# One Trainium2 core, mLSTM and a mixture of experts: other zero products ahead of the first expert step, chunk 2 read and normed ahead of the fourth step

## The chip, the cores and the metric

The kernel runs on one core of a Trainium2 chip. The metric is the time of one execution in microseconds (us). The engines' names are those of the profile: PE is TensorE (PEld its weight loads), DVE is VectorE, ACT is ScalarE, POOL is GpSimd, SP is the engine that issues the DMA transfers here.

## The reference: what is computed

Two parts in a row, all float32. The first is an mLSTM over batch 2, 8 heads, 768 positions, head size 40, written as a recurrence:

```
m_new = maximum(f_t + m, i_t)
f_stab, i_stab = exp(f_t + m - m_new), exp(i_t - m_new)
C = f_stab * C + i_stab * outer(v_t, k_t);  n = f_stab * n + i_stab * k_t
y_t = sigmoid(o_t) * (C q_t) / maximum(|n . q_t|, 1)
```

The second takes the result as 1536 tokens of width 320 and sends every token through 4 experts with hidden width 1024:

```
p = domain_probs / (domain_probs.sum(-1) + 1e-9)
out = sum over e of p[:, e] * (maximum(x @ w1[e], 0) @ w2[e])
```

## The kernel before, in words

The sequence is cut into 12 chunks of 128 tokens; chunk `n` is batch `n % 2`, position block `n // 2`. In a chunk the recurrence is matrix work:

- `scores(n)` (L447): k times q on TensorE, into two PSUM tiles `s`. `decay(n)` (L416): two DVE scans that make the decay matrix `dd` from a broadcast of the forget gates, `fb`. For chunks 0 to 3 `fb` is made on TensorE into PSUM by `spread(n)` (L399); from chunk 4 on it is loaded into SBUF from a DRAM copy by `load_f(n)` (L409). `weigh(n)` (L453, DVE): scores times decay, `pm`.
- `inter(n)` (L494): q times the state `cs` carried from the chunk before, into a PSUM tile, and 8 ACT copies `yb` (L501). `intra(n)` (L509): `pm` times the values `vp`, into another. `norm(n)` (L522 to L529, DVE): adds both, divides and gates.
- `state(n)` (L465): the chunk's addition to the state; `carry(n)` (POOL, L481) decays the old one, L475 (DVE) adds. `values(n)` (L428 ACT, L430 POOL) and `keys(n)` (L436 POOL) make its operands.
- `turn(n)` (L536): three transposes, and ACT copies (L538, L539) into the experts' input `xst`; `turn_lo(n)` (L543, L544, DVE) the rests.

Float32 products of the experts are made from parts in a shorter format: each weight and each input is split into a high part (`split_hi`, L96, ACT) and a low rest (`split_lo`, L99, POOL or DVE), and TensorE adds up products of the parts.

The first of the 4 experts runs while the attention does. The class `Expert` holds a list of steps for a group of 256 tokens: 4 steps `hidden` (L164: 16 products into one PSUM bank, then relu and rest, L173 and L174) and then the steps `output` (L203). For the first group the output of each of its two token blocks is cut in two: the part with the high half of `w2` (16 products) and the part with the low half (8 products), in the order high 0, high 1, low 0, low 1. `steps(n)` runs the next `n` steps. The order of everything is written out by hand: each engine takes its instructions in the order of the code, and waits by semaphores only. `SLOTS` gives, for each chunk from 2 on, how many steps run before `inter(n + 1)`, before `turn(n)` and after `turn_lo(n)`.

The code from L554 to L676 is a prelude for chunks 0 and 1. It begins with the gates: scans and exponentials on 16 partitions; `gate_t` (L329) transposes them with TensorE, `gate_b` (L306) is a long DVE scan, `gate_last` and `gate_l` (L351) give the factors `bl` (L355) for the carried states. The first four `hidden` steps are spread over the prelude, L643, L649, L665 and L674. The loop from L678 does chunks 2 to 11.

`keep_warm(n)` (L75) is a product of 128 x 128 zeros with `n` columns of zeros; nothing reads it.

PSUM tiles come from pools of two buffers taken in turn. `gate_t`, `intra`, `inter`, `state` and the later `turn` share the pool `ps_y`: each takes the buffer that the tile two before it had, and waits until that one has been read. The scores and some zero products share `ps_w`. The SBUF pool `a0` for the loaded `fb` takes the place of the gates' pool `gp` (L668), tile by tile when the gates have been read.

Of the kernel before, what the change touches and what calls it, by code (L numbers as in the profile page):

```python
# [10 lines left out]
AF = mybir.ActivationFunctionType  # L11
# [7 lines left out]
L = 128  # L19
# [16 lines left out]
NPE = 4  # L36

SLOTS = (
    (0, 1, 1), (1, 1, 0), (0, 2, 0), (1, 1, 0), (1, 1, 0),
    (1, 1, 0), (1, 1, 0), (1, 1, 0), (1, 2, 0), (1, 1, 1),  # L40
)
PAD = 56
# [6 lines left out]
def tile_mlstm_moe(ctx, tc, gt, qk, vk, ot, dp, w1, w2, out):  # L49
    ctx.enter_context(tc.manual_schedule())  # L50
    nc = tc.nc
# [20 lines left out]
    def keep_warm(n, pool=ps_h, tag="ph"):  # L72

        pwm = pool.tile([L, n], F32, tag=tag, name="pwm")
        nc.tensor.matmul(pwm, zero[:, 0:L], zero[:, 0:n], start=True, stop=True)  # L75

    for _ in range(WARM):
        keep_warm(512)
    keep_warm(256)

    def copy(eng, dst, src):
        if eng is nc.scalar:
            eng.activation(dst, src, AF.Copy)
        else:
            eng.tensor_copy(dst, src)
# [9 lines left out]
    def split_hi(hi, raw):  # L95
        nc.scalar.activation(hi, raw, AF.Copy)  # L96
# [11 lines left out]
    def split_w2_hi(ws, f0, n, raw):  # L108
        f = slice(f0, f0 + n)
        split_hi(ws[:, HI, f], raw[:, f])  # L110
# [111 lines left out]
    with ExitStack() as actx:  # L222
# [4 lines left out]
        w1s, w2s = new_weights(0)  # L227
# [24 lines left out]
        ps_y = actx.enter_context(tc.tile_pool(name="ps_y", bufs=2, space=PSUM))  # L252
# [4 lines left out]
        BH = B * H  # L257
        gat = gp.tile([BH, 2, S], F32, name="gat")
# [4 lines left out]
        ib = gp.tile([L, S], F32, name="ib")  # L263
# [55 lines left out]
        def gate_t(c0, c1):  # L319

            pit = pits[c0] = ps_y.tile([L, 512], F32, tag="y", name="pit")
            n = c1 - c0
            po = n * 48
            if c0:
                g = slice(c0 * L, c1 * L)
                nc.scalar.activation(ib[32:32 + BH, g], gat[:, 0, g], AF.Copy)
            for c in range(c0, c1):
                o = (c - c0) * 48
                nc.tensor.matmul(  # L329
                    pit[:, o:o + 48], ib[:, c * L:(c + 1) * L], ident[:, 0:48],  # L330
                    start=True, stop=True,
                )
            nc.scalar.activation(
                ibT[:, c0:c1], pit[:, 0:po].rearrange("t (c g) -> t c g", c=n), AF.Copy
            )
# [77 lines left out]
        def decay(n):  # L413
            dds[n] = a1.tile([L, H, L], F32, tag=f"dd{n % 2}", name="dd")
            for i in range(2):
                nc.vector.tensor_tensor_scan(  # L416
                    out=dds[n][:, 4 * i:4 * i + 4].rearrange("p h t -> p (h t)"),
                    data0=fbs[n][i].rearrange("p h t -> p (h t)"),
                    data1=id4.rearrange("p h t -> p (h t)"),
                    initial=0.0, op0=ALU.mult, op1=ALU.add,  # L420
                )
# [19 lines left out]
        def scores(n, pool=ps_w, tag="w"):  # L441
            ss[n] = [pool.tile([L, NP, L], F32, tag=tag, name="s") for _ in range(2)]
            qg, kg = qT(n), kT(n)
            for p in range(NP):
                for r in range(2):
                    q = slice(64 * r, 64 + D * r)
                    nc.tensor.matmul(ss[n][r][:, p, :], kg[q, p], qg[q, p], start=True, stop=True)  # L447
# [29 lines left out]
        def carry(n):  # L477
            b, c = n % B, n // B
            if 0 < c < NC - 1:
                cd = cds[n] = a1.tile([104, NP, L], F32, tag=f"cd{b}", name="cd")  # L480
                nc.gpsimd.tensor_mul(  # L481
                    cd, cs[b][0:104],
                    bl[0:104, c, b * NP:(b + 1) * NP].unsqueeze(2).to_broadcast([104, NP, L]),
                )

        def inter(n, pool=ps_y, tag="y"):

            b, c = n % B, n // B
            if c == 0:
                return  # L490
            y1 = pool.tile([L, H, 64], F32, tag=tag, name="y1")
            for p in range(NP):
                for t in (slice(0, 64), slice(64, L)):
                    nc.tensor.matmul(  # L494
                        y1[t, 2 * p:2 * p + 2, :].rearrange("t r d -> t (r d)")[:, 0:65 + D],
                        qT(n)[:, p, t], cs[b][0:104, p, 0:65 + D], start=True, stop=True,
                    )
            yb = ybs[n] = a1.tile([L, H, D + 1], F32, tag=f"yb{n % 2}", name="yb")
            for h in range(H):
                i = 32 + b * H + h  # L500
                nc.scalar.activation(  # L501
                    yb[:, h], y1[:, h, 0:D + 1], AF.Copy, scale=ibT[:, c, i:i + 1]
                )

        def intra(n):
            y = y0s[n] = ps_y.tile([L, H, 64], F32, tag="y", name="y0")
            for h in range(H):
                for t in (slice(0, 64), slice(64, L)):
                    nc.tensor.matmul(  # L509
                        y[t, h, 0:D + 1], pms[n][:, h, t], vvs[n][:, h, 0:D + 1],  # L510
                        start=True, stop=True,
                    )

        def norm(n):

            y, xr = y0s[n], a1.tile([L, H, D], F32, tag=f"xr{n % 2}", name="xr")
            xrs[n] = xr.rearrange("t h d -> t (h d)")
            yd, yn = y[:, :, 0:D], y[:, :, D:D + 1]
            nq = a1.tile([L, H, 1], F32, tag="nq", name="nq")
            na, ni = y[:, :, D + 2:D + 3], y[:, :, D + 4:D + 5]  # L520
            if n // B:
                nc.vector.tensor_add(y[:, :, 0:D + 1], y[:, :, 0:D + 1], ybs[n])  # L522
            nc.vector.tensor_scalar(
                out=nq, in0=yn, scalar1=-1.0, scalar2=1.0, op0=ALU.mult, op1=ALU.max
            )
            nc.vector.tensor_mul(xr, yd, ogs[:, n])  # L526
            nc.vector.tensor_tensor(out=na, in0=yn, in1=nq, op=ALU.max)
            nc.vector.reciprocal(ni, na)
            nc.vector.tensor_mul(xr, xr, ni.to_broadcast([L, H, D]))  # L529
# [18 lines left out]
        def steps(n):  # L548
            for _ in range(n):
                if not work[0].step():  # L550
                    work.pop(0)
# [36 lines left out]
        nc.scalar.activation(even, par.unsqueeze(2).to_broadcast([L, 2, 64]), AF.Copy)  # L588
        gate_max(1, NC)
        spread(0, ps_h, "ph")  # L590
        for _ in range(2):
            keep_warm(256, ps_w, "w")
        scores(0)
        gate_t(0, 1)
# [1 line left out]
        g1, m1, mp1 = slice(L, S), mb[:, L + 1:S + 1], mb[:, L:S]  # L596
# [5 lines left out]
        decay(0)  # L602
        nc.gpsimd.tensor_sub(fs[:, g1], fs[:, g1], m1)
        nc.scalar.activation(fs[:, g1], fs[:, g1], AF.Exp)
        scores(1, ps_h, "ph")
        weigh(0)
        decay(1)
# [6 lines left out]
        w2r = raws.tile([L, NF, DM], F32, tag="raw", name="w2r")  # L614
        nc.sync.dma_start(w2r, w2[0])
        load_vk(1)
        load_o(1)
        for _ in range(3):
            keep_warm(256, ps_w, "w")
        weigh(1)  # L620
        quarter_hi(0)
# [19 lines left out]
        gate_b(1, NC)  # L641
        gate_last(1, NC)
        steps(1)  # L643
        decay(2)
        scores(2)
        state(0)
# [18 lines left out]
        steps(1)  # L665
        gate_l(1, NC)
        carry(2)
        gctx.close()  # L668
        a0 = actx.enter_context(
            tc.tile_pool(name="a0", bufs=1, side="right", reuse_waits="tile")  # L670
# [2 lines left out]
        load_f(NPE + 1)  # L673
        steps(1)  # L674
        nc.vector.reciprocal(psum_e, psum_e)
        inter(2)  # L676

        for n in range(2, NCH):  # L678
            j, cc = n // 2, n % 2
            k = SLOTS[n - 2]  # L680
            nxt = n + 1 < NCH
            if cc == 0 and j + 1 < NG:
                load_qk(j + 1)
                load_vk(j + 1)
            if NPE + 1 < n + 2 < NCH:
                load_f(n + 2)
            if cc == 0:
                if j > 1:
                    gate_o(j)
                if j + 1 < NG:  # L690
                    load_o(j + 1)
            if n == NCH - 2:
                raw1 = load_w1e(1)
            if n > 3 and nxt:
                decay(n + 1)
            steps(k[0])
            if nxt:
                inter(n + 1)
            intra(n)
            norm(n)  # L700
            if n == 2:
                for f in (4, 6):
                    split_w2_hi(w2s, f, 2, w2r)
            if nxt:
                scores(n + 1)
            state(n)
            if nxt:
                values(n + 1)
                if n == 2:
                    for f in (4, 6):  # L710
                        split_w2_lo(w2s, f, 2, w2r, nc.gpsimd)
                    nc.gpsimd.tensor_mul(pw, pw, psum_e.to_broadcast([L, NCH, NE]))
                keys(n + 1)
                weigh(n + 1)
                carry(n + 1)
            steps(k[1])
            turn(n)
            if n == 2:
                decay(4)
            turn_lo(n)  # L720
            steps(k[2])
# [109 lines left out]
```

## Time and profile before

| | |
|---|---|
| time, median of 3 runs | 411.47 us (408.71 to 411.73) |
| the profiled execution | 413.55 us |
| its span, first to last instruction | 411.7 us |
| TensorE busy | 402.6 us (98%) |
| DVE, ACT, POOL busy | 174.1, 125.4, 85.0 us |
| mean granted clock of TensorE | 0.988 |
| relu copies L173 on ACT, 96 of them | 598 ns mean |

Times in the views are counted from the start of the span. The granted clock is the share of TensorE's full speed that was granted in a stretch: 1.00 or, at its lower level, 0.50. In the chain of waits every piece is what the end of the program was waiting for at that time: an engine with the operation and its line, a transfer, or "issue", which is time in which the engine waited for nothing that the profile shows. In the timelines a bracket after a row gives how long the engine had been idle before it and what released it. "x16" is the number of instructions merged in a row; a product of float32 data is recorded as two.

### The profile page before, as it was taken

How to read it: one execution, taken by the hardware profiler on the slowest of the kernel's cores; microseconds unless marked ns; L12 is line 12 of the kernel's file. 1: busy time of each engine (PE TensorE's matmuls, PEld its weight loads, DVE VectorE, ACT ScalarE, POOL GpSimd, SP SyncE). 2: the span in 40 equal slices, each digit the busy share in tenths (PEclk: the TensorE clock that was granted, in tenths of full speed). 3: DMA queues.
4: the chain of work that ended last, by engine and by line, in shares of the span. 5: the costliest groups of instructions: out<-in, count | busy, mean ns of one | idle time of the engine just before them, and what ended most of it. 6: DMA issues, size and time to landing. Idle time of an engine off the chain costs nothing.

```text
span 411.7 us, 7167 instructions
## 1 busy us (share of the span) xinstructions
PE 402.6 (98%) x3046; PEld 365.3 (89%) x3046; DVE 174.1 (42%) x312; ACT 125.4 (30%) x298; POOL 85.0 (21%) x97
## 2 busy tenths in 40 slices
PE   8989999999999999999999999999999999999996
PEld 5778989999998898998988988989989889899896
DVE  7683699699762403313214234133142251231321
ACT  4657434353323533205214032033030140220210
POOL 4865932222012620003410010016100010000000
PEclk9698999999999999999999999999999999999999
DMA  6964967545000213000300004002000000001001
GB/s 174 306 228 110 240 175 222 150 134 206 2 2 2 77 52 116 37 2 0 129 0 2 0 2 153 2 0 90 40 0 2 0 2 32 33 0 49 17 18 48
DMA packets 14883, 29.34 MB, mean 71 GB/s; under 512 B 987, under 2 KB 10747, under 8 KB 13435
## 3 DMA queue, kind: packets, MB, share of 16 engines
q1 hardware_dynamic: 14851, 28.88, 22.3%
q8 instruction: 24, 0.39, 0.4%
q14 instruction: 8, 0.07, 0.1%
HBM read 26.86 MB, written 2.02 MB: 70 GB/s over the span
## 4 chain that ended last, share of the span: by engine, by line
PE 94%; DMA 2%; DVE 1%; issue 1%; SPq 1%; ACT 0%; ACTq 0%
PE po L203 41%; PE ph L164 40%; PE y L509 3%; PE s L447 3%; PE ph L186 3%; DMA qk<-in_qk 2%; PE y L494 2%; PE st L465 1%; PE px L536 1%; PE pwm L75 1%; PE pit L329 0%; SPq L555 0%; PE fb L399 0%; DVE pm L453 0%; DVE xr L526 0%
## 5 line engine op out<-in xcount | busy, mean ns | idle before, releaser
L203 PE MATMUL po<-w2s,h 128*128 128x320 f32 x1152 | 172.8, 310 | 0.0
L203 PEld LDWEIGHTS po<-w2s,h 128*128 128x128 f32 x1152 | 169.7, 188 | 1.0
L164 PE MATMUL ph<-xst,w1s 128*128 128x512 f32 (+1 forms) x816 | 165.6, 361 | 0.0
L164 PEld LDWEIGHTS ph<-xst,w1s 128*128 128x128 f32 x816 | 137.2, 191 | 24.8 <-issue 2.4
L173 ACT ACTIVATE h<-ph 128x512 fp32r<-128x512 f32 x96 | 57.4, 598 | 200.6 <-PE ph L164 200.6
L174 DVE SCALAR_TENSOR_TENSOR h<-ph,h 128x512 fp32r<-128x512 f32 x96 | 66.2, 689 | 104.0 <-ACT h L173 103.5
L213 DVE SCALAR_TENSOR_TENSOR acc<-po,pw,acc 128x320 f32<-128x320 f32 x36 | 19.8, 550 | 99.9 <-PE po L203 99.9
L99 POOL TENSOR_TENSOR w1s<-raw,w1s 128x512 fp32r<-128x512 f32 (+1 forms) x24 | 23.6, 1023 | 74.4 <-ACT w1s L96 67.4
L99 POOL TENSOR_TENSOR w2s<-raw,w2s 128x640 fp32r<-128x640 f32 x6 | 9.5, 1577 | 98.2 <-ACT w2s L96 98.2
L416 DVE TENSOR_TENSOR_SCAN dd<-fb,id 128x512 f32<-128x512 f32 x24 | 28.0, 1208 | 1.8 <-PE fb L399 1.6
L211 ACT ACTIVATE acc<-po,pw 128x320 f32<-128x320 f32 x12 | 6.3, 528 | 34.7 <-PE po L203 34.7
L501 ACT ACTIVATE yb<-y,ibT 128x41 f32<-128x41 f32 x80 | 15.8, 317 | 2.6 <-PE y L494 2.2
L447 PE MATMUL s<-qk 64*128 64x128 f32 x192 | 14.9, 297 | 1.5 <-DMA qk<-in_qk 1.5
L453 DVE TENSOR_TENSOR pm<-s,dd 128x512 f32<-128x512 f32 x24 | 15.4, 686 | 1.4 <-PE s L447 1.1
L509 PEld LDWEIGHTS y<-vp,pm 128*64 128x64 f32 x384 | 13.3, 145 | 3.0 <-issue 2.1
L509 PE MATMUL y<-vp,pm 128*64 128x41 f32 x384 | 14.0, 235 | 1.7 <-issue 1.0
L447 PEld LDWEIGHTS s<-qk 64*128 64x128 f32 x192 | 12.5, 199 | 2.5 <-PE pwm L75 1.1
L436 POOL TENSOR_TENSOR kp<-vk,dd 128x320 f32<-128x320 f32 x10 | 8.2, 827 | 29.5 <-DVE dd L416 29.5
L96 ACT ACTIVATE w2s<-raw 128x640 fp32r<-128x640 f32 x12 | 8.8, 733 | 16.2 <-DMA raw<-in_w 16.2
L186 PE MATMUL ph<-xd,w1s 64*128 64x512 f32 x40 | 12.0, 420 | 0.0
L186 PE MATMUL ph<-xst,w1s 64*128 64x512 f32 x40 | 11.9, 417 | 0.0
L430 POOL TENSOR_TENSOR vp<-vk,ibT 128x320 f32<-128x320 f32 x12 | 8.7, 724 | 13.9 <-PE st L465 9.0
(90 smaller groups left out, 205.8 us busy)
## 6 DMA issues: line engine op xcount, KB each, us to landing
raw<-in_w SPq DMA_DIRECT2D x3, 1536.0 KB, 6.4
qk<-in_qk SPq DMA_DIRECT2D x5, 832.0 KB
fb<-f_d SPq DMA_DIRECT2D x8, 512.0 KB, 3.9
raw<-in_w SPq DMA_DIRECT2D x3, 1280.0 KB
vk<-in_vk SPq DMA_DIRECT2D x5, 640.0 KB, 8.2
acc<-in_ot SPq DMA_DIRECT2D x6, 320.0 KB, 8.1
out<-acc SPq DMA_DIRECT2D x12, 160.0 KB, 1.8
w2r<-in_w SPq DMA_DIRECT2D x1, 1280.0 KB
```

The lines of the kernel that those rows point to most:

```text
L99: eng.tensor_sub(lo, raw, hi.bitcast(F32))
L164: nc.tensor.matmul(ph[:, i, :], self.w1s[:, wi, f * L:(f + 1) * L], xst[:, xi, self.t0:self.t0 + n], start=(k == 0 and not self.wide), sto ...
L173: nc.scalar.activation(hh, ph, AF.Relu)
L174: nc.vector.scalar_tensor_tensor(out=hl, in0=ph, scalar=0.0, in1=hh.bitcast(F32), op0=ALU.max, op1=ALU.subtract)
L186: nc.tensor.matmul(self.banks[f][:, 0, :], self.w1s[r, 5, f * L:(f + 1) * L], x, start=True, stop=False,)
L203: nc.tensor.matmul(po, self.hs[f][a][:, sl], ws[:, b, f, :], start=(first and i == 0), stop=(last and i == len(ks) - 1),)
L213: nc.vector.scalar_tensor_tensor(out=acc[:, i, :], in0=po, scalar=pw[:, i, e:e + 1], in1=acc[:, i, :], op0=ALU.mult, op1=ALU.add,)
L416: nc.vector.tensor_tensor_scan(out=dds[n][:, 4 * i:4 * i + 4].rearrange("p h t -> p (h t)"), data0=fbs[n][i].rearrange("p h t -> p (h t)") ...
L447: nc.tensor.matmul(ss[n][r][:, p, :], kg[q, p], qg[q, p], start=True, stop=True)
L453: nc.vector.tensor_mul(pm[:, r], ss[n][r], dd[:, r])
L501: nc.scalar.activation(yb[:, h], y1[:, h, 0:D + 1], AF.Copy, scale=ibT[:, c, i:i + 1])
L509: nc.tensor.matmul(y[t, h, 0:D + 1], pms[n][:, h, t], vvs[n][:, h, 0:D + 1], start=True, stop=True,)
```

## The change

It makes these edits:

- Zero products: one of 128 columns is added behind the first ones at the start; three instead of two of 256 columns stand ahead of `scores(0)`; one of 256 columns, in the pool `ps_y`, is added ahead of `scores(1)`; two instead of three stand ahead of `weigh(1)`.
- The ACT copy of the scanned gates into `ib` leaves `gate_t` and stands right behind the first `hidden` step.
- `inter(2)`, `intra(2)` and `norm(2)` move ahead of the fourth `hidden` step and of the loads `load_f(4)` and `load_f(5)`; `inter(3)` moves behind `state(2)`.
- ACT's high halves of `w2` for the hidden blocks 4 to 7 move from behind `norm(2)` to behind the fourth step.
- The slots: chunk 2 runs one output part before `turn(2)` (high 0) and none after; chunk 3 runs none before `inter(4)`, one before `turn(3)` (high 1) and two after `turn_lo(3)` (low 0, low 1).

```diff
 SLOTS = (
-    (0, 1, 1), (1, 1, 0), (0, 2, 0), (1, 1, 0), (1, 1, 0),
+    (0, 1, 0), (0, 1, 2), (0, 2, 0), (1, 1, 0), (1, 1, 0),
     (1, 1, 0), (1, 1, 0), (1, 1, 0), (1, 2, 0), (1, 1, 1),
 )
...
     keep_warm(256)
+    keep_warm(128)
...
-            if c0:
-                g = slice(c0 * L, c1 * L)
-                nc.scalar.activation(ib[32:32 + BH, g], gat[:, 0, g], AF.Copy)
             for c in range(c0, c1):
...
         spread(0, ps_h, "ph")
-        for _ in range(2):
+        for _ in range(3):
             keep_warm(256, ps_w, "w")
         scores(0)
...
+        keep_warm(256, ps_y, "y")
         scores(1, ps_h, "ph")
...
-        for _ in range(3):
+        for _ in range(2):
             keep_warm(256, ps_w, "w")
         weigh(1)
...
         steps(1)
+        nc.scalar.activation(ib[32:32 + BH, g1], gat[:, 0, g1], AF.Copy)
         decay(2)
...
         carry(2)
+        inter(2)
+        intra(2)
+        norm(2)
         gctx.close()
...
         nc.vector.reciprocal(psum_e, psum_e)
-        inter(2)
+        for f in (4, 6):
+            split_w2_hi(w2s, f, 2, w2r)
 
         for n in range(2, NCH):
...
             steps(k[0])
-            if nxt:
-                inter(n + 1)
-            intra(n)
-            norm(n)
-            if n == 2:
-                for f in (4, 6):
-                    split_w2_hi(w2s, f, 2, w2r)
+            if n > 2:
+                if nxt:
+                    inter(n + 1)
+                intra(n)
+                norm(n)
             if nxt:
                 scores(n + 1)
             state(n)
+            if n == 2:
+                inter(3)
             if nxt:
                 values(n + 1)
```

## Rows read from the trace of the kernel before

**Rows 1.** Stretches: sum, PE, PEld, DVE, ACT, POOL busy, granted clock, DMA share, GB/s

```profile
11.00:17.50 6.50, 6.19 (x54) 5.45 (x54) 4.45 (x9) 5.47 (x9) 5.46 (x9) 0.50 0.98 322
17.50:18.00 0.50, 0.50 (x4) 0.06 (x4) 0.00 (x0) 0.00 (x0) 0.50 (x2) 0.73 1.07 258
18.00:31.00 13.00, 11.41 (x143) 10.10 (x143) 9.91 (x16) 5.92 (x16) 9.28 (x13) 1.00 0.72 233
31.00:31.50 0.50, 0.50 (x7) 0.50 (x6) 0.00 (x0) 0.50 (x2) 0.08 (x1) 0.93 0.00 0
31.50:34.50 3.00, 3.00 (x16) 3.00 (x15) 2.34 (x2) 2.97 (x4) 3.00 (x4) 0.50 0.00 0
```

**Rows 2.** The chain of waits, 0 to 50 us: start, length, what

```profile
3.18 8.00 DMA qk<-in_qk
...
11.31 2.08 PE s L447 x16
...
15.26 2.75 PE pwm L75 x6
18.01 1.09 PE y L509 x32
...
20.17 0.50 DVE xr L529
...
21.73 2.45 PE ph L164 x16
...
32.10 3.23 PE ph L164 x16
...
35.47 1.98 PE ph L164 x16
...
39.05 1.02 issue
...
42.30 0.43 PE st L465 x16
...
45.60 3.52 PE po L203 x24
49.12 0.87 PE y L494 x16
```

**Rows 3.** The timeline, TensorE's rows: start, length, engine, line, operation

```profile
29.62 1.31 PE L329 MATMUL pit<-ident,ib 128*128 128x48 f32 x10 [1.51 <-ACT ib L326]
...
55.70 1.13 PE L509 MATMUL y<-vp,pm 128*64 128x41 f32 x32 [0.70 <-DVE xst L544]
```

**Rows 4.** The timeline, DVE's rows

```profile
10.40 2.33 DVE L416 TENSOR_TENSOR_SCAN dd<-fb,id 128x512 f32<-128x512 f32 x2
...
22.64 2.44 DVE L306 TENSOR_TENSOR_SCAN gat<-fs,bs 16x640 f32<-16x640 f32 x1
...
43.31 0.66 DVE L475 TENSOR_TENSOR cs<-cd,st 40x164 f32<-40x164 f32 x2
44.00 1.29 DVE L453 TENSOR_TENSOR pm<-s,dd 128x512 f32<-128x512 f32 x2
...
47.89 0.28 DVE L544 TENSOR_TENSOR xst<-px,xst 64x128 fp32r<-64x128 f32 x1
```

**Rows 5.** The timeline, ACT's rows

```profile
34.55 0.20 ACT L428 ACTIVATE vp<-ibT 128x8 f32<-128x8 f32 x1
...
45.91 0.26 ACT L539 ACTIVATE xst<-px 64x128 fp32r<-64x128 f32 x1
```

**Rows 6.** The timeline, POOL's rows

```profile
17.08 0.71 POOL L99 TENSOR_TENSOR w1s<-wb,w1s 64x256 fp32r<-64x256 f32 x1
...
23.69 1.91 POOL L99 TENSOR_TENSOR w1s<-wb,w1s 64x256 fp32r<-64x256 f32 x1
```

**Rows 7.** The timeline, issues of transfers by SP

```profile
9.08 0.33 SPq L376 DMA_DIRECT2D qk<-in_qk  x1
...
35.93 0.55 SPq L376 DMA_DIRECT2D qk<-in_qk  x1
```

## The prediction

> **What bounds the kernel now.** I read the clock by stretches first, then the chain of waits, then the engines' timelines around its gaps. [...] What the engine did before each fall: before the first it had stood waiting for q and k of chunk 1, whose transfer lands at 11.18 (3.18 + 8.00) [rows 2]; before the second it had stood 1.51 us, until 29.62, for the ACT copy of `ib` [rows 3]. From about 60 us on the chain is matrix products end to end and the diff changes none of that work. So the change is worth what it takes out of the first 56 us: TensorE's waits, and work done at the lower level. Four waits stand there: for the transfer, for `ib` (the products of `gate_t` start late), 1.02 us at 39.05 (`intra(2)`, whose PSUM buffer is that of `inter(2)`, still being read by ACT) [rows 2], and 0.70 us before 55.70 (`intra(4)`, whose buffer `turn_lo(3)` frees) [rows 3].
>
> **The change, part by part.** All times are of the profiled execution: 413.55 us, a span of 411.7 and 1.85 around it. The median shown is 2.1 us less; I take the saving over whole.
>
> *Zero products.* Added: 128 columns at the start, 256 before `scores(0)`, 256 before `scores(1)`; one of 256 behind `intra(0)` goes. The three that stand there now take 2.75 us at the lower level [rows 2], so 0.92 each, and 0.46 at the upper. The first three stand in places where TensorE waits for data in any case (`fr`; the two transfers of q and k, the second of which lands at 11.18): cost 0, or at most 0.1 to 0.2 if one runs at the lower level. What they may do is hold the clock over 11.18. At the upper level `scores(1)` takes 1.04 (half of 2.08) and ends at 12.35. What is late next is DVE: the scan `decay(1)` ends at 12.73 [rows 4], `weigh(1)` takes 1.29 to 14.02, and TensorE has done `intra(0)` (1.09, as the other `intra` at 18.01) and two zero products (0.92) by 14.4 and `intra(1)` by 15.5. A norm takes 1.57 (from 19.10, where the second `intra` ends, to 20.67, where L529 does) [rows 2]: `norm(0)` ends at 15.59, `norm(1)` at 17.16. From its end to the first expert step are 1.06 now (20.67 to 21.73): the step starts at 18.22. The step's weights (POOL's low half of the first quarter, behind ACT's high half) are there at 17.79 [rows 6], since neither engine waits for TensorE before that, so they are not later. **Gain 3.5 us** (0.5 if the clock does not hold: the dropped product saves 0.92 and the one before `scores(1)` costs some 0.1, the rest goes in the order of DVE).
>
> *A transfer and POOL, next.* `scores(2)` moves from 24.18 (where 21.73 + 2.45 ends) to 20.7. Its q and k were issued at 9.08 [rows 7]; no row gives their landing, only that nothing waited at 24.18. With the 8.00 us of the other such transfer they would be there at 17.1; the wait is between 0 and 3.5. Also the scan L306 moves from 22.64 to some 19 us, onto POOL's lows and keys. Beside it one L99 took 1.91 instead of 0.71 [rows 6], and itself took 2.44, where 640 columns at the rate of `decay(1)` (2.33 for 1024) would take 1.46, so 0.9 to 1.0 more [rows 4]: they hold each other up, and `state(1)` needs POOL's keys. That is 0 to 1.2. The two delays stand at one place and overlap; nearer the short ends I take **a loss of 0.6**.
>
> *The copy of `ib`* goes ahead of decay, scores and the second step. It needs L306, some 21.5, when ACT is free. So `gate_t` follows the second step without a wait: the 1.51 before 29.62 go [rows 3], **1.5 us gained**. With no wait ahead, the fall of the clock at 31.5 should go: the third step takes 3.23 at the lower level, its neighbour 1.98 [rows 2]: **1.25 gained**; 0 if it falls anyway.
>
> *Chunk 2 ahead of the fourth step.* ACT becomes the bound for a moment. From the end of `gate_t`'s products (29.62 + 1.31 = 30.93) to the end of L428 (34.55 + 0.20) ACT is busy 3.8 us with `ibT`, weight halves, a table load and the sigmoid [rows 3, 5]; then come the third step's relu (0.60, in the table of times) and the small copy `bl`, of about L428's 0.20, that frees the PSUM buffer of `intra(2)`: 4.6. TensorE's own way there is what stood from 30.93 to 35.47 (`spread(3)`, the third step, `gate_l`) less 1.25, and `inter(2)` (0.87, as `inter(4)`): 4.2. It waits some 0.5, where 1.02 stood before: **0.5 gained** (between -0.5 and 1.0). `norm(2)` on DVE then lies beside the fourth step. `inter(3)` behind `state(2)` needs the buffer that `norm(2)` has long freed. The weight halves 4 and 6 on ACT now stand behind the fourth relu and before `inter(3)`'s copies, and are there for the output part.
>
> *Output parts behind chunk 3's reads.* Between `turn(2)` and `intra(3)` stood 24 output products (3.52) and `inter(4)` (0.87) [rows 2]; now only `inter(4)` does, and `intra(3)` takes the buffer that `turn_lo(2)` frees on DVE, behind `decay(4)`. Count from the end S of `scores(3)` (42.30 now). TensorE does what takes 3.30 now (`state`, 16 output products, `turn(2)`, to 45.60), with `inter(3)` (0.87) added ends `turn(2)` at S + 4.2, and `inter(4)` at S + 5.0. ACT's copies of `turn(2)` take from 45.60 to 46.17 [rows 5], so 0.6, and `turn_lo(2)` some 0.7: S + 5.5 at the earliest. DVE's own way is `state` (0.43), the sums L475 (0.66), and then what runs from 44.00 to 48.17 without a gap, `weigh(3)`, `decay(4)` and `turn_lo(2)` [rows 4]: S + 5.3. So the wait is 0.5 if nothing holds DVE up. But POOL's low halves of w2 now run where `decay(4)` starts; `decay(4)` is a scan of two SBUF tensors as L306 is, and L306 was held up 0.9 by POOL. That puts DVE at S + 6.2: **a loss of 1.2** (between 0.5 and 2.5, where a second such hold-up comes and one more in `turn_lo`). In return 16 output products stand between `turn(3)` and `intra(4)`, and its wait of 0.70 goes: **0.7 gained**.
>
> [...]
>
> *Transfers.* q and k of chunk 4 are issued at 35.93 now [rows 7], right behind `gate_l` (35.47), and used at 49.12, 13.2 us later. After the change the issue still follows `gate_l`; `inter(4)` comes some 10 us behind it. The 8.00 us of the first transfer fits. Cost 0; 3 if it needed all 13.
>
> **Sum:** 3.5 - 0.6 + 1.5 + 1.25 + 0.5 - 1.2 + 0.7 = 5.65 us. 413.55 - 5.65 = 407.9 profiled, and 411.47 - 5.65 = **405.8** as the median.
>
> **Rivals.**
> *The clock is not held at 11 us* (or most executions of the kernel before have no such fall, since the median is 2.1 us under the profiled one). For it: between 9 and 18 us most products are narrow or of few rows, so busy time may flatter what the engine does. The gain of 3.5 becomes 0.5: **408.8**. [...]
> *All is hidden:* no hold-up by POOL, q and k in time, `intra(3)` waits 0.5: 5.65 + 0.6 + 0.7 = 6.95, **404.5**. For it: the decay in [rows 4] (2.33 for a pair) shows no hold-up; but that one reads PSUM.
> *The moved norm holds the loads:* the loads behind the memory freed after `norm(2)`, or slow transfers, make `inter(4)` wait. If q and k are issued only when `norm(2)` ends, 5 us later, it waits some 3: **408.8**. Against it: the freed tiles are not those of chunk 2.
> *The other side: the low level lasts.* In the kernel before the clock rises within 17.5 to 18.0 [rows 1], when the zero products (15.26 to 18.01) have just run. One of them is gone. If the clock falls at 11 as before and does not rise until the next place where it moves now (31.4, in the stretch with 0.93), 13.6 us of work at half speed cost 6.8, against a remaining gain of 5.65 - 3.0 = 2.65: 411.47 + 4.15 = **415.6**. It is slower than before from 5.3 us of extra low clock on. Against it: after 34.5 the clock rose behind expert products alone [rows 1, 2], and such products start at 18 to 21 us after the change.
>
> **How the numbers follow.** Forecast 0.48, clock not held 0.20, all hidden 0.14, loads 0.08, low level lasts 0.10. The range is 403.5 to 410.0: the second and fourth cases and the hidden one with 1 us about them; outside lie the low level (0.10) and some 0.08 of tails. 1% is 4.1 us, about what a measurement of this kernel tells from no change; faster than 407.4 are some four fifths of the forecast (0.38), the hidden case (0.14) and a little of the others (0.04): 0.56. Slower than 415.6 is half of the last case and a tail, 0.06. Same: 0.38.
>
> **What would show it.** Right: clock 1.00 from 9 to 31.5 us and beyond; first expert step near 18.2; `gate_t` without a wait; about 0.5 us of wait before `intra(2)`, 0.5 to 1.2 before `intra(3)`, none before `intra(4)`; that `intra(4)` starts near 50 instead of 55.70. Wrong: a clock of 0.50 anywhere past 10 us; `scores(2)` waiting over 1 us for its transfer; `inter(4)` waiting for q and k.

## The result, and the profile after: 408.66 us, 0.9914 of the time before

The changed kernel takes 408.66 us (median of 20 runs, 407.55 to 415.69) and the kernel before 412.33 us beside it (20 runs, 408.71 to 415.98): a ratio of 0.9914, 95% interval 0.9894 to 0.9933, or some 3.6 us less. Forecast were 405.8 us and a saving of 5.65; 408.66 lies in the range, in its slower half. The likeliest outcome of the prediction, faster than 407.4 us (0.56), did not come; the band that did had 0.38. The profile that came with this result (run after) had caught one of the 4 executions in 20 that took 415.65 to 415.69 us (of the kernel before 3 in 20 took 415.82 to 415.98), and in it the products up to 24 us ran at about half speed (`intra(0)` and `intra(1)` took 1.94 and 1.89 us; in the profile before `intra(0)` took 1.93 at a clock of 0.50, `intra(1)` 1.13 at mostly 1.00), so the rows of after are those of a second profile of the same kernel (run after_again: 407.63 us, span 405.8, the quickest of that run's nine executions).

The clock by stretches in that profile (columns as in [rows 1]): no lower level anywhere, where [rows 1] have 0.50 from 11.0 to 17.5 and from 31.5 to 34.5.

```profile
11.00:13.00 2.00, 2.00 (x45) 1.79 (x45) 1.90 (x3) 1.97 (x3) 2.00 (x2) 1.00 1.05 407
13.00:16.00 3.00, 2.87 (x53) 2.34 (x49) 2.84 (x9) 2.99 (x6) 2.23 (x7) 1.00 1.00 336
16.00:18.00 2.00, 2.00 (x16) 1.60 (x15) 1.55 (x6) 1.22 (x6) 2.00 (x3) 1.00 0.96 218
...
30.00:36.50 6.50, 5.95 (x99) 5.55 (x100) 4.49 (x12) 4.18 (x16) 4.68 (x5) 1.00 0.87 222
```

Its timeline, TensorE's rows (the lines of the code have shifted: L165 is the expert step that was L164, L445 the scores, L327 `gate_t`, L507 `intra`):

```profile
18.11 2.44 PE L165 MATMUL ph<-xst,w1s 128*128 128x256 f32 x16
...
21.01 1.16 PE L445 MATMUL s<-qk 64*128 64x128 f32 x16 [0.46 <-DMA qk<-in_qk]
...
24.85 1.21 PE L327 MATMUL pit<-ident,ib 128*128 128x48 f32 x10
...
30.55 1.13 PE L507 MATMUL y<-vp,pm 128*64 128x41 f32 x32 [0.60 <-POOL w2s L100]
...
41.26 1.13 PE L507 MATMUL y<-vp,pm 128*64 128x41 f32 x32 [1.46 <-DVE xst L542]
...
49.83 1.08 PE L507 MATMUL y<-vp,pm 128*64 128x41 f32 x32
```

The bracket of `intra(2)` at 30.55 names POOL's low half of `w2`, which does not write its buffer. What frees that buffer is, as forecast, ACT's small copy `bl`, through at 30.44:

```profile
30.25 0.19 ACT L353 ACTIVATE bl<-pit 128x40 f32<-128x40 f32 x1
```

These rows answer [rows 2, 3]. The first expert step starts at 18.11 instead of 21.73. `gate_t` has no bracket any more: its 1.51 us of wait are gone. Three waits are left, each where the prediction put one: 0.46 before `scores(2)`, 0.60 before `intra(2)` (1.02 before), and a new one of 1.46 before `intra(3)`. `intra(4)` starts at 49.83 without a wait; in [rows 3] it was 55.70 with 0.70. So the 5.9 us between the two spans (411.7 and 405.8) are all made by that point, and nothing is given back later. What has to be explained is why the medians differ by only 3.7.

### The profile page after: what moved, and what is told of

It reads as the page before. It is cut to its first block, busy times and chain, and to the rows that moved or that the text cites. A ratio compares the mean times of both kernels' runs of the same rounds, so it can differ in the third digit from the quotient of the medians.

```text
span 413.9 us, 7180 instructions
## 1 busy us (share of the span) xinstructions
PE 407.7 (99%) x3050; PEld 369.0 (89%) x3050; DVE 175.5 (42%) x312; ACT 125.3 (30%) x298; POOL 84.8 (20%) x97
## 4 chain that ended last, share of the span: by engine, by line
PE 97%; DVE 2%; issue 0%; DVEq 0%
PE po L204 40%; PE ph L165 39%; PE s L445 4%; PE y L507 3%; PE pwm L75 3%; PE ph L187 3%; PE y L492 2%; PE fb L397 1%; PE st L463 1%; PE px L534 1%; DVE dd L414 1%; PE pit L327 0%; DVE pm L451 0%; DVE cs L473 0%; DVE acc L214 0%
## 5 line engine op out<-in xcount | busy, mean ns | idle before, releaser
L165 PE MATMUL ph<-xst,w1s 128*128 128x512 f32 (+1 forms) x816 | 164.4, 359 | 0.0
L165 PEld LDWEIGHTS ph<-xst,w1s 128*128 128x128 f32 x816 | 135.9, 189 | 24.8 <-issue 2.4
L414 DVE TENSOR_TENSOR_SCAN dd<-fb,id 128x512 f32<-128x512 f32 x24 | 28.9, 1244 | 1.0 <-PE fb L397 0.8
L507 PEld LDWEIGHTS y<-vp,pm 128*64 128x64 f32 x384 | 14.0, 152 | 3.4 <-POOL kp L434 1.6
L507 PE MATMUL y<-vp,pm 128*64 128x41 f32 x384 | 14.8, 242 | 2.1 <-DVE xst L542 1.5
L445 PE MATMUL s<-qk 64*128 64x128 f32 x192 | 15.9, 310 | 0.0
L445 PEld LDWEIGHTS s<-qk 64*128 64x128 f32 x192 | 13.4, 210 | 2.0 <-issue 0.7
L434 POOL TENSOR_TENSOR kp<-vk,dd 128x320 f32<-128x320 f32 x10 | 8.2, 825 | 31.6 <-DVE dd L414 31.6
L75 PE MATMUL pwm<-const-float32-0.0 128*128 128x256 f32 (+2 forms) x24 | 12.3, 663 | 0.8 <-PEq L816 0.8
```

Of the source, the lines that this page charges most:

```text
L165: nc.tensor.matmul(ph[:, i, :], self.w1s[:, wi, f * L:(f + 1) * L], xst[:, xi, self.t0:self.t0 + n], start=(k == 0 and not self.wide), sto ...
L414: nc.vector.tensor_tensor_scan(out=dds[n][:, 4 * i:4 * i + 4].rearrange("p h t -> p (h t)"), data0=fbs[n][i].rearrange("p h t -> p (h t)") ...
L507: nc.tensor.matmul(y[t, h, 0:D + 1], pms[n][:, h, t], vvs[n][:, h, 0:D + 1], start=True, stop=True,)
```

## The experiments

The ratios below are to the kernel before, run on the same chip beside each; where I subtract us from a ratio, I take 412 us for it. The brackets are 95% intervals. In diffs the kernel before is the base for zero_only and ib_only, tl_first for tl_qk, and the changed kernel for the rest.

**after_again.** The changed kernel, unaltered.

> The changed kernel once more. If the saving of 3.6 us is real it stays at 0.991 of the kernel before. In an undisturbed profile I expect products at half speed (a 256-column zero product 0.85 to 0.95 us) only in the first 4 to 5 us, gate_t without a wait, and a wait of about 1.5 us before intra(3). The rival, that the saving is a matter of when the clock happens to rise, expects profiles with half-speed products past 11 us in about half of the executions of either kernel.

0.992 (0.9892 to 0.9948), 408.86 us: the saving stands. Of the profile all three expectations came: half speed only in the zero products at the start, no wait at `gate_t`, and 1.46 us before `intra(3)`. The rival expected half-speed products past 11 us in about half of the executions of either kernel. The mean granted clock, which is on record for each execution, says otherwise: it is 0.999 or 1.000 in all nine here, and below 0.997 in most executions of the kernel before (the table further down).

**zero_only, ib_only, order_only.** The three groups of edits one at a time. zero_only:

```diff
+    keep_warm(128)
...
-        for _ in range(2):
+        for _ in range(3):
             keep_warm(256, ps_w, "w")
         scores(0)
...
+        keep_warm(256, ps_y, "y")
         scores(1, ps_h, "ph")
...
-        for _ in range(3):
+        for _ in range(2):
             keep_warm(256, ps_w, "w")
         weigh(1)
```

> The kernel before with the zero products of the change alone. Predicted: 3.5 us faster than before, 0.9915, if they hold the clock over the transfer at 11 us. Rival (they don't hold it, or it falls seldom in the kernel before): 0 to 0.5 us, 0.999 to 1.000.

0.9961 (0.993 to 0.9992), 1.6 us less. That is between the two theories: the forecast 0.9915 lies outside the interval, the rival's 0.999 just inside. Its timeline (TensorE) and clock show both halves of the answer:

```profile
18.52 2.45 PE L165 MATMUL ph<-xst,w1s 128*128 128x256 f32 x16
22.68 2.06 PE L448 MATMUL s<-qk 64*128 64x128 f32 x16 [1.71 <-DMA qk<-in_qk]
...
29.69 1.31 PE L330 MATMUL pit<-ident,ib 128*128 128x48 f32 x10 [1.51 <-ACT ib L327]
...
31.75 2.13 PE L165 MATMUL ph<-xst,w1s 128*128 128x256 f32 x16
```

```profile
13.00:16.00 3.00, 2.86 (x63) 2.33 (x59) 2.74 (x9) 2.99 (x6) 2.23 (x7) 1.00 1.00 338
...
22.50:26.50 4.00, 3.82 (x52) 3.55 (x53) 3.90 (x6) 0.98 (x4) 4.00 (x6) 0.57 0.97 379
```

The clock is held past 11 us and the first step starts at 18.52, 3.2 us earlier than in the profiled execution before. Then `scores(2)` stands 1.71 us for q and k, the clock falls behind that wait (0.57 from 22.5 to 26.5), and `gate_t` still waits 1.51 for `ib`. By then the whole head start is gone: `gate_t` starts at 29.69, in [rows 3] at 29.62. What this execution keeps (a span of 410.3 against 411.7) comes from the third step, which ran at the upper level, in 2.13 us where [rows 2] have 3.23.

ib_only:

```diff
-            if c0:
-                g = slice(c0 * L, c1 * L)
-                nc.scalar.activation(ib[32:32 + BH, g], gat[:, 0, g], AF.Copy)
...
         steps(1)
+        nc.scalar.activation(ib[32:32 + BH, g1], gat[:, 0, g1], AF.Copy)
         decay(2)
```

> The kernel before with the early ib copy alone. Predicted: 1.5 us of wait gone and 1.25 of half-speed step, together 2.75 us, 0.9933. Rival: the wait alone, 1.5 us, 0.9964, with the low clock at 31 us still there or elsewhere.

0.9957 (0.9918 to 0.9996), 1.8 us less: the wait of 1.51 and a little, nearer the rival, though the interval holds both figures. In its profile no clock falls near 31 us (1.00 from 22.5 to 60), but one still falls at 11 (0.56 from 11.0 to 13.0, 0.50 from there to 18.0).

order_only: the move of chunk 2, the slots and the weight halves, with the zero products and the copy of `ib` as before.

> The kernel before with chunk 2 ahead of the fourth step, the moved output parts and weight halves alone. By the predicted terms (0.5 - 1.2 + 0.7) 0 us, 1.000. A wait of 0.5 to 1.6 us before intra(3), none before intra(4). Rival (POOL holds decay(4) up twice): 1 us slower, 1.0025.

1.0017 (0.998 to 1.0055): no difference that can be told. The sum of the three terms (1.000) and the rival (1.0025) both lie in the interval, so the times don't choose. In its profile `intra(3)` waits 1.47 us, as in the changed kernel, and nothing stands before `intra(4)`, as forecast.

**tl_first.** The new wait before `intra(3)` was the largest loss, so its two suspected causes were taken apart: the place of `decay(4)` in DVE's order here, POOL's share in the next run.

```diff
             turn(n)
+            turn_lo(n)
             if n == 2:
                 decay(4)
-            turn_lo(n)
```

> The changed kernel with turn_lo(2) ahead of decay(4) on DVE. If the wait before intra(3) (1.46 us in the fast profile of the changed kernel) comes from decay(4) standing ahead, intra(3) starts when the copies of turn(2) and turn_lo(2) are through, about 1.0 us earlier: a wait of 0.45, and 0.9 us off the time (0.9978 of the changed kernel) if decay(4), now later, is not awaited by weigh(4). Rival: decay(4) becomes late for POOL's keys and weigh(4), and the us comes back before state or intra of the next chunk: no change.

0.9897 (0.9859 to 0.9935), 407.75 us. The intervals of this and of the changed kernel overlap, so the gain between the two is not shown by the times. The profile shows the mechanism. In the changed kernel (after_again), DVE's and POOL's rows:

```profile
37.33 3.17 DVE L414 TENSOR_TENSOR_SCAN dd<-fb,id 128x512 f32<-128x512 f32 x2
...
38.24 1.18 POOL L716 TENSOR_TENSOR pw<-pw,psum_e 128x48 f32<-128x48 f32 x1
...
39.39 1.65 POOL L434 TENSOR_TENSOR kp<-vk,dd 128x320 f32<-128x320 f32 x1
```

and in tl_first, with the row of `intra(3)` on TensorE last:

```profile
38.21 0.27 POOL L716 TENSOR_TENSOR pw<-pw,psum_e 128x48 f32<-128x48 f32 x1
38.44 0.73 POOL L434 TENSOR_TENSOR kp<-vk,dd 128x320 f32<-128x320 f32 x1
...
39.51 0.42 DVE L541 TENSOR_TENSOR xst<-px,xst 128x256 fp32r<-128x256 f32 x1 [2.12 <-ACT xst L537]
...
40.26 2.34 DVE L414 TENSOR_TENSOR_SCAN dd<-fb,id 128x512 f32<-128x512 f32 x2
40.37 1.13 PE L507 MATMUL y<-vp,pm 128*64 128x41 f32 x32 [0.60 <-DVE xst L542]
```

The wait before `intra(3)` falls from 1.46 to 0.60, near the 0.45 expected. And what had been beside each other before is now apart: the two scans take 2.34 instead of 3.17, the small product L716 0.27 instead of 1.18, the keys L434 0.73 instead of 1.65. One reordering shortened operations on both engines, and no work was taken away.

**hi_early.** POOL's low halves of w2 moved away from `decay(4)`.

```diff
         norm(2)
+        for f in (4, 6):
+            split_w2_hi(w2s, f, 2, w2r)
         gctx.close()
...
         nc.vector.reciprocal(psum_e, psum_e)
-        for f in (4, 6):
-            split_w2_hi(w2s, f, 2, w2r)
```

> The changed kernel with ACT's high halves of w2 blocks 4 to 7 ahead of the fourth step's relu (ACT stood idle there 1.9 us), so that POOL's low halves run some 1.7 us earlier and end before decay(4) starts. If POOL holds decay(4) up, its two scans take 2.33 us again instead of 3.17, and the wait before intra(3) falls from 1.46 to about 0.6. Rival, that decay(4) is long for another reason (its input comes from SBUF): 3.17 stays and so does the wait.

0.9907 (0.9873 to 0.9941). The expectation missed: `decay(4)` became longer, not shorter, and the wait before `intra(3)` rose to 1.79. Its DVE and POOL rows tell why:

```profile
33.96 3.06 POOL L100 TENSOR_TENSOR w2s<-w2r,w2s 128x640 fp32r<-128x640 f32 x2
...
37.22 0.73 POOL L434 TENSOR_TENSOR kp<-vk,dd 128x320 f32<-128x320 f32 x1
37.46 3.50 DVE L414 TENSOR_TENSOR_SCAN dd<-fb,id 128x512 f32<-128x512 f32 x2
...
37.92 1.95 POOL L479 TENSOR_TENSOR cd<-cs,bl 104x512 f32<-104x512 f32 x1
```

The low halves are through at 37.02, as meant. But POOL went straight on to the keys and to the carry L479, which takes 1.95 here against 1.04 in tl_first, where no scan runs beside it. So the two scans were long beside two different kinds of POOL's work: 3.50 here beside the keys and the carry, 3.17 in the changed kernel beside the low halves (in run after these end at 46.34 and the scans start at 45.39), L716 and the keys. In tl_first POOL stood idle from 40.18 to 42.14, and the scans from 40.26 on took 2.34; the rival (long because its input is in SBUF) doesn't explain that, as the scan of tl_first reads the same tile. They were not long beside all of POOL's work, though: in the profile before, the small product (L712 there) started with them and took 1.26, the keys took 1.65, and the scans 2.35:

```profile
45.21 2.35 DVE L416 TENSOR_TENSOR_SCAN dd<-fb,id 128x512 f32<-128x512 f32 x2
...
45.22 1.26 POOL L712 TENSOR_TENSOR pw<-pw,psum_e 128x48 f32<-128x48 f32 x1
...
46.45 1.65 POOL L436 TENSOR_TENSOR kp<-vk,dd 128x320 f32<-128x320 f32 x1
```

**both.** The two edits together.

> Both edits. The copies of turn(2) set the start of intra(3): a wait of 0.45, as with the order of turn_lo alone; together 1.0 us faster than the changed kernel (about 0.9976 of it).

0.9922 (0.9889 to 0.9955). The wait before `intra(3)` is 0.60, near the 0.45 expected. The total isn't better, and its profile, of an execution of 410.34 us, shows what else varies:

```profile
23.09 1.58 PE L445 MATMUL s<-qk 64*128 64x128 f32 x16 [1.73 <-DMA qk<-in_qk]
```

Here q and k of chunk 2 arrive 2 us later than in after_again, and behind that wait the clock is lower (0.65 from 22.5 to 26.5, 0.92 from 26.5 to 30.0). The eleven executions fall in two groups: five with a mean granted clock of 0.996, as in this profile, took 409.9 to 410.3 us, the six with 0.999 or 1.000 took 406.4 to 409.0.

**ib_order.** The changed kernel with the zero products of before.

> The changed kernel with the zero products of the kernel before. If the zero products hold the clock they are worth here what they are worth alone (1.6 us), so 0.995 to 0.996 of the kernel before, and a half-speed stretch past 11 us in the profile. Rival: the other edits alone already give 0.992, the zero products add nothing.

0.9964 (0.9933 to 0.9995): near the 0.995 to 0.996 expected, and the rival (0.992 without them) lies outside the interval. Ten of its twelve executions have a mean granted clock of 0.990 to 0.996; of the changed kernel's 26 in the table below, one has. The clock in its profile, with a fall that no profile with all the new zero products shows at that place:

```profile
11.00:13.00 2.00, 2.00 (x34) 1.78 (x34) 1.90 (x3) 1.60 (x2) 2.00 (x3) 0.70 1.04 402
13.00:16.00 3.00, 3.00 (x25) 2.56 (x24) 2.29 (x7) 2.99 (x6) 1.77 (x6) 0.50 0.97 332
16.00:18.00 2.00, 2.00 (x25) 1.35 (x25) 0.00 (x0) 0.44 (x2) 2.00 (x3) 0.50 1.06 223
```

**no_gap.** The changed kernel without the one product ahead of `scores(1)`.

```diff
-        keep_warm(256, ps_y, "y")
         scores(1, ps_h, "ph")
```

> The changed kernel without the one zero product ahead of scores(1). TensorE then waits some 0.5 us before scores(1). If that product holds the clock, the profile shows a stretch at 0.50 from about 11 us (zero products behind intra(0) at 0.92 each instead of 0.46), a first expert step at 19.5 or later instead of 18.1, and 0.995 to 0.996 of the kernel before. Rival: the third product ahead of scores(0) is enough; then no fall and 0.992.

0.9911 (0.9881 to 0.994), no slower than the changed kernel; the time went with the rival. The profile went with the theory, with a first step at 19.91 and this clock:

```profile
12.50:15.50 3.00, 3.00 (x35) 2.74 (x36) 2.79 (x8) 2.97 (x5) 2.32 (x6) 0.50 1.01 383
```

Both can be true. Four of the twelve executions, the profiled one among them, have a mean granted clock of 0.990 to 0.996, the other eight 0.998 to 1.000. With the product one of 26 has less than 0.998. So it seems to matter in some executions and not in most; its worth is below what these times tell apart.

**tl_qk.** The kernel of tl_first with q and k of chunks 2 and 3 requested ahead of the second half of w1.

```diff
         load_w1(0)
-        load_w1(1)
         load_qk(1)
+        load_w1(1)
```

> The changed kernel with turn_lo(2) ahead of decay(4) and with the transfer of q and k of chunks 2 and 3 ahead of the second half of w1. The wait of scores(2) for its transfer (0.46 us in one profile, 1.73 in another) should go; with the clock held 0.5 to 1.5 us less than with turn_lo alone, 0.986 to 0.989 of the kernel before. Rival: the second half of w1 comes later instead, ACT's and POOL's quarters 2 and 3 move back and the third step waits: same or slower than turn_lo alone.

0.9862 (0.9822 to 0.9901), 407.47 us against 407.75 of tl_first: the two aren't told apart. No wait stands before `scores(2)`, as in the profile of tl_first, and another came, of the rival's kind (ACT's third quarter of `w1` waited for its transfer until 21.76, and so its copies of `ib` and `cs` behind it came late):

```profile
25.59 1.31 PE L327 MATMUL pit<-ident,ib 128*128 128x48 f32 x10 [0.81 <-ACT cs L84]
```

This and tl_first have the lowest medians of the study; both are below the changed kernel's, though not beyond the intervals.

**before_copy1, before_copy2.** The kernel before, for more profiles of it.

> The kernel before, for a second profile of it. If the predicted saving was too large because other executions of the kernel before have fewer half-speed stretches, this one shows only one of the two (at 11 us or at 31 us) and a span of 407 to 410 us. Rival: both stretches again, a span near 411.7.

> The kernel before once more, for a third profile, as for the second one.

They took 411.88 and 414.07 us, with spans of 410.1 and 412.3. The clock of the first, and its waits on TensorE (who waited, for what, us in total, times, longest):

```profile
13.00:16.00 3.00, 3.00 (x46) 2.49 (x43) 2.51 (x9) 2.99 (x6) 2.03 (x6) 1.00 0.99 346
...
22.50:26.50 4.00, 3.96 (x53) 3.69 (x54) 3.86 (x5) 1.23 (x4) 3.92 (x7) 0.58 0.99 376
```

```profile
PE s L447 <- DMA qk<-in_qk: 2.2, 2, 1.8
PE pit L329 <- ACT ib L326: 1.5, 1, 1.5
```

and the clock of the second:

```profile
13.00:16.00 3.00, 3.00 (x17) 2.24 (x14) 2.18 (x7) 2.99 (x6) 2.03 (x6) 0.50 0.99 342
...
30.00:36.50 6.50, 6.50 (x32) 6.50 (x32) 2.96 (x3) 4.42 (x8) 4.93 (x5) 0.50 0.00 0
```

In the first the clock does not fall at 11 us although nothing in the kernel is changed; its first step starts at 18.32, as early as after the change. It then waits 1.77 us for q and k, and the clock falls at 23. The second has both falls of [rows 1], the later one twice as long. The wait for `ib` is 1.51 in both.

## Why the prediction was right, and which step made it too large

*The terms, against the second profile of the changed kernel.* In that one quick execution they hold one by one. First step: 18.22 forecast, 18.11 found. Transfer and POOL before `scores(2)` and `state(1)`: a loss of 0.6 forecast, 0.46 of wait found, and by the transfer alone (none in tl_first and hi_early, 1.73 in the run both, so how near it came is partly luck); the longer scan did come (L307, the L306 of before, took 3.15 us instead of 2.44, beside POOL's keys and low halves of `w1`) but delayed no one on the path. `ib`: the wait of 1.51 gone, the third step 2.1 us instead of 3.23. `intra(2)`: 0.5 forecast, 0.60. `intra(3)`: 1.2 forecast, 1.46 found. `intra(4)`: no wait, near 50 forecast, 49.83 found. Sum 5.65 forecast; the spans differ by 5.9.

*The step that failed* is the first one of the working: "The median shown is 2.1 us less; I take the saving over whole." The two places at the lower level, worth 3.5 + 1.25 of the 5.65, aren't a fixed part of the kernel before. Of six profiles with the old zero products (the one before, its two copies, ib_only, order_only, ib_order) four fall between 10.9 and 13 us, two don't. Of six with all the new ones (after_again, zero_only, tl_first, hi_early, both, tl_qk) none does; a seventh, of the execution of 415.65 us, had no upper level to fall from. So the zero products do hold the clock there, but a part of the executions had it for nothing. The mean granted clock of every execution on record under 415 us says how large that part is (kernel before: those run beside the experiments; changed kernel: run after and after_again). It tells that the clock fell, not where, and it leaves out half speed at the start (0.999 in the 415.65 us of run after; last section).

| kernel | executions | mean granted clock | time, us | median, us |
|---|---|---|---|---|
| before | 6 | 1.000 | 408.2 to 409.4 | 409.1 |
| before | 24 | 0.992 to 0.996 | 411.0 to 412.4 | 411.7 |
| before | 25 | 0.982 to 0.988 | 412.7 to 414.8 | 413.2 |
| changed | 25 | 0.999 or 1.000 | 407.6 to 409.7 | 408.6 |
| changed | 1 | 0.996 | 410.7 | |

The execution from which the prediction was worked out (0.988, 413.55 us) is of the third kind, which is less than half of the 55. Against that kind the changed kernel saves 4.6 us, against the second 3.1, and against the first 0.5. The terms without the two for the clock add up to 0.9 (5.65 - 3.5 - 1.25). So by these groups the change is worth in the main the falls of the clock that it takes out, and 5.65 was the price for an execution that had both of them.

The rival "the clock is not held" named this in its bracket and gave it 408.8. That this is nearly the measured 408.66 is luck: its mechanism, that the change fails to hold the clock, did not come; only the half of its reason that stands in the bracket did.

The profiled executions themselves stand apart from their medians: the one before (413.55) is 1.2 us above the median of 20 (412.33), the one after (407.63) 1.0 below its own (408.66), and 5.9 - 1.2 - 1.0 = 3.7 is only this subtraction. For the 1.2 the table shows the reason. For the 1.0 the likely reason is the transfer of q and k of chunk 2: it ended the wait at 21.0 us in after_again, at 21.75 in order_only and at 23.1 in the run both, which also lost the clock behind it. One profile each can't give its share, so that remains argued.

*The three groups* measured alone give 1.6 + 1.8 - 0.7 = 2.7 us, and together 3.3 to 3.5 (0.992 and 0.9914); with intervals of over 1 us each the difference is not a finding. ib_order against the changed kernel (0.9964 to 0.9914) puts the zero products at some 2 us in company, with intervals that just touch.

*The rivals.* "All is hidden" fell: the wait before `intra(3)` was 1.46, not 0.5. That POOL is a cause is shown from both sides, by tl_first (the scans took 2.34 with POOL idle beside most of them) and by hi_early (3.50 beside its keys and carry). How the two hold each other up was not shown; measured is that L716 took 1.18 beside a scan and 0.27 without one. "The moved norm holds the loads" fell: q and k of chunk 4 were issued at 29.52, behind `gate_l` and before `norm(2)`, and `inter(4)` waited for nothing. "The low level lasts" came at its price but not by its path: the execution in the profile of run after took 415.65 us, forecast were 415.6, but its products ran at half speed from the start to 24 us, where the rival has a fall at 11 and no rise until 31. As the kernel before has executions of 415.8 to 416.0 us too, it is not shown that the change brings them.

## What to carry to other kernels

The terms of a sum can all be right and the total too large, when the profiled execution holds events that other executions don't: before a stretch at the lower clock is booked as a gain, look at more profiles of the kernel before, and book only the share of them that shows it. The mean granted clock of every timed execution gives that share without a profile. A wait that moves out of the way uncovers the next one at once; here the transfer of q and k, which nothing had waited for in the profile before, took up to 1.7 us of a head start of 3.5. And when a step is moved off TensorE's path, check who stands ahead of it in its engine's order: `turn_lo(2)` needed 0.7 us and waited behind a scan of 3.2.

## What the runs showed of the hardware that was not expected

The granted clock reads 1.00 over the first 5 us in every profile, but the first zero products take nearly as long as at the lower level: in after_again's chain of waits 1408 columns take 4.62 us (3.3 ns each), the next 768 columns 1.50 us (2.0 each). At a clock of 0.50, 768 such columns took 2.75 us (3.6 each) in [rows 2].

```profile
0.78 4.62 PE pwm L75 x8
...
6.43 1.50 PE pwm L75 x6
```

In run after the clock's column reads 1.00 up to 24 us as well, while these 768 columns take 2.93 us (3.8 ns each); its clock and its row in the timeline:

```profile
9.00:11.00 2.00, 2.00 (x8) 1.19 (x8) 0.22 (x1) 0.00 (x0) 0.00 (x0) 1.00 1.00 330
```

```profile
7.63 2.93 PE L75 MATMUL pwm<-const-float32-0.0 128*128 128x256 f32 x6
```

At the start of these profiles the durations of equal products show the lower speed, and the clock's column doesn't. The other surprise is how long one engine's small operation becomes beside the other's scan: 1.18 us (after_again) for 48 columns on POOL that took 0.27 in tl_first, with DVE's scans taking 0.8 us more in the same stretch (3.17 and 2.34).
